# A decode of float64 weights with one Vector instruction fewer, and a hand-over between two MLPs begun earlier, in a fused attention and MLP kernel

## The chip, the cores and the metric

One core of one Trainium2 chip runs the whole program. The metric is the device time of one execution in microseconds. The engines are named as in the profile: PE is the matrix engine, DVE the vector engine, ACT the scalar engine, POOL the GpSimd engine, and SP the engine that does nothing here but issue DMAs. Each of them works through its own list of instructions strictly in the written order, so an instruction that waits holds back all that is written behind it on its engine.

## The reference

A softmax attention without a score matrix feeds two MLPs. Weights arrive as float64; activations are float32.

```python
def _attn_ref(q, k, v):                 # 8 batches, 8 heads, 576 tokens, 64 wide
    q_s = softmax over the last axis of q
    k_s = softmax over the tokens of k
    kv = np.einsum('bhsd,bhse->bhde', k_s, v)
    return np.einsum('bhsd,bhde->bhse', q_s, kv)

def _moe_ref(x, w_gate, w_val, w_out, rms_g):   # 4608 tokens, 512 -> 1536 -> 512
    xn = x / np.sqrt(np.mean(x * x, axis=-1, keepdims=True) + 1e-06) * rms_g
    g = xn @ w_gate
    return (g * (1 / (1 + np.exp(-g))) * (xn @ w_val)) @ w_out

def _moe2_ref(x, w_in, w_out):                  # 4608 tokens, 512 -> 2048 -> 512
    h = x @ w_in
    return (h * (1 / (1 + np.exp(-1.702 * h)))) @ w_out
```

## The kernel before

**Stages.** (1) The attention of the first batch and the first weights. (2) Nine tiles of 512 tokens through the first MLP (index j); inside each tile the attention of later batches is woven in. A tile has 36 slots, three for each of the 12 blocks of the hidden width: a gate product, a value product, and an output product of the block before. (3) The first product of the second MLP (`in_round`): six units of 768 tokens, four rounds each. (4) Its second product: nine groups of 512 tokens, eight steps of the hidden width each; the loop over `k` counts all 72. The products of the second MLP are done with seven instead of eight block products, so each operand is first turned into seven sums and differences (`sums`, line 570), and each of the seven is split into a high and a low part: ACT copies the high part, DVE or POOL subtracts to get the low one.

**Decoding.** A weight is a float64, read as two 32 bit words. `decode` (lines 136 to 157) takes the absolute value of the high word on ACT (line 148), scales the low word on ACT (149), then on DVE clips from below (150), shifts left by three and masks (151), and puts sign and top bit back (154); POOL adds the low word (157). There are 68 pieces of 128x512. `advance` decodes 36 of them, three before and 33 during tile 0, beside which POOL also makes the low parts (line 161). A piece passes through one of three `stage` buffers; its next fetch is issued by SP only when POOL has added the low word. The other 32 pieces, for the second MLP, are decoded in tiles 1 to 7 (`decode_aside`) and parked in DRAM.

**Order in tile 0.** In the DVE list decoding stands between the attention's steps. The step that matters to PE is line 411 (`qL`): it reads a PSUM bank that PE's transpose at line 328 waits for, and behind that transpose stand the output product (line 526) and all that follows.

**The hand-over from stage 3 to stage 4.** `beside[i, t]` holds what is to be done after PE's block number t of unit i. In the last unit (END) the factors of step k=0 (`u2_split(0)`) are made after block 25: ACT copies the high part (line 739) out of `aside`, DVE subtracts (742). They lie where the factors of the first five of a round's seven block products lay (`pools["x"]`), which are last read in block 25. Block 26 and 27 follow with two additions on DVE, two GELUs on ACT and two stores on SP each. Only then come the loads of step 3 and of the last weights (`y`), the sums of step 1, and its split. The data of steps 4 and 5 are loaded behind those.

**The end.** The last group's four tiles of 128 tokens are y2 (i = 0, 1) and y1 (i = 0, 1). DVE finishes them with seven additions, and DMAs store whole rows of 512.

Of the kernel before, what the change touches and what calls it, by code (L numbers as in the profile page):

```python
# [20 lines left out]
def attention_glu_mlp(  # L21
# [90 lines left out]
    def f(x):  # L112
        return x.bitcast(F32)
# [22 lines left out]
    def decode(name, dst):  # L136

        st = stages.pop(name)
        lo, hi = st[:, :, 0], st[:, :, 1]


        nc.scalar.activation(f(dst), f(hi), AF.Abs)
        nc.scalar.activation(lo, lo.bitcast(U32), AF.Copy, scale=2.0**-29)
        nc.vector.tensor_scalar_max(f(dst), f(dst), 2.0**-15)  # L150
        nc.vector.tensor_scalar(  # L151
            dst, dst, 3, 0x3FFFFFF8, op0=ALU.logical_shift_left, op1=ALU.bitwise_and
        )
        nc.vector.scalar_tensor_tensor(
            out=dst, in0=hi, scalar=-0x40000000, in1=dst, op0=ALU.bitwise_and, op1=ALU.bitwise_or
        )
        return lambda: nc.gpsimd.tensor_tensor(dst, dst, lo, op=ALU.add)  # L157

# [475 lines left out]
        halve(w[:, 0], w[:, 1], xraw2[i, c][:, RIGHT[p]], nc.vector)  # L634
        xfac[i, p, c] = w

    def in_round(i, q, after):


        sets = (2 * q, 2 * q + 1)  # L640
        st = {m: {} for m in sets}

        def gelu(m, k, dst, src):
            nc.scalar.activation(dst, src, AF.Gelu_apprx_sigmoid)  # L644
            nc.sync.dma_start(out=u2_d[i][m][:, k], in_=dst)

        def room():
            return pools["h"].tile([P, W], F32, tag="h", bufs=12, name="h")

        for p in ORDER:  # L650
            for s, m in enumerate(sets):
                d = st[m]
                if p in (1, 6, 5):
                    d[p] = pools["ps"].tile([P, 512], F32, tag="bank", bufs=8, name="ps_in")
                t = d[{1: 1, 2: 1, 6: 6, 7: 6, 4: 6, 5: 5, 3: 5}[p]][:, 0:W]
                w = wpack["2i", q, p]
                for c in range(2):
                    for k, (a, e) in enumerate(PASSES):
                        nc.tensor.matmul(  # L659
                            t,  # L660
                            w[:, a, s, c * P : (c + 1) * P],
                            xfac[i, p, c][:, e, :],
                            start=p in (1, 6, 5) and c == 0 and k == 0,
                            stop=c == 1 and k == 2,
                            skip_group_check=True,
                        )
                if p == 1:
                    d["c1"] = room()
                    nc.scalar.activation(d["c1"], t, AF.Copy)
                elif p == 6:  # L670
                    d["u2"] = room()
                    nc.vector.tensor_tensor(d["u2"], d["c1"], t, op=ALU.add)
                elif p == 2:
                    gelu(m, 2, room(), t)
                elif p == 7:
                    d["u3"] = room()
                    nc.vector.tensor_tensor(d["u3"], d["c1"], t, op=ALU.add)
                else:
                    k, name = {5: (1, "u3"), 4: (3, "c1"), 3: (0, "u2")}[p]
                    v = d[name]  # L680
                    nc.vector.tensor_tensor(v, v, t, op=ALU.add)  # L681
                    gelu(m, k, v, v)
            after(ORDER.index(p))
# [3 lines left out]
        unit, o = divmod(2 * g + i, W // P)  # L687
        return unit, o * P, (2 * unit + h) * W + o * P

    def store_out(first, y, queue=nc.scalar):  # L690

        done = 0
        while done < P:
            b, o = divmod(first + done, S)
            rows = sum(halves_of(b), [])
            while o >= size(rows[0]):
                o -= size(rows.pop(0))
            m = min(P - done, size(rows[0]) - o)
            if rows[0] < R - 1:
                dst = out[b * S : b * S + FULL].rearrange("(p r) e -> r p e", p=P)[rows[0]]  # L700
            else:
                dst = out[b * S + FULL : (b + 1) * S]
            queue.dma_start(out=dst[o : o + m, :], in_=y[done : done + m, :])
            done += m


# [22 lines left out]
        if k in uraw:  # L729
            sums(uraw[k], "A", (nc.vector,) * 4)  # L730

    def u2_split(k, ahead=True):

        if k not in uraw:
            return
        raw = uraw.pop(k)[:, 1:8]
        pool, bufs = (pools["u"], 2) if k % 3 < 2 else (pools["d"], 1)
        w = pool.tile([P, 2, 7, Q], F32R, tag="uf", bufs=bufs, name="uf")
        nc.scalar.activation(w[:, 0], raw, AF.Copy)  # L739
        if ahead:  # L740
            u2_sums(k + 1)
        nc.vector.tensor_tensor(w[:, 1], raw, f(w[:, 0]), op=ALU.subtract)  # L742
        ufac[k] = w

    def warm(func):

# [3 lines left out]
    with tc.manual_schedule():  # L750
# [187 lines left out]
            pools["x"].release()  # L938
            pools["u"] = tc.alloc_tile_pool(name="u2p", bufs=1, side="right", reuse_waits="tile")

        beside[END, 25].insert(0, free_x)
        beside[END, 25].insert(1, lambda: u2_split(0, False))
        put2(END, 25, lambda: u2_load(2))
        for i in range(NUNIT):
            for q in range(4):

                def after(k):
                    for fn in beside.pop((i, 7 * q + k), ()):
                        fn()

                in_round(i, q, after)


        pools["h"].release()
# [4 lines left out]

            return dpool.tile([P, 8, Q], F32, tag="y", bufs=2, name="y")  # L960

        assert not beside
        u2_load(3)

        work = {}
        for m in (6, 7):
# [2 lines left out]

            for k, part in ((m - 4, a[1:2]), (2 * m - 9, a[2:6]), (2 * m - 8, a[6:])):  # L970
                work.setdefault(k, []).extend(part)
        u2_sums(1)
        u2_split(1, False)
        u2_sums(2)
        for k in range(4, 6):
            u2_load(k)
        stores = []
        for k in range(NT // T * NSET):
            g, m = divmod(k, NSET)
# [22 lines left out]
            for p in (1, 6, 7, 5, 3, 4, 2):  # L1002
# [21 lines left out]
                elif p == 6:  # L1024
                    add(u2, c1)
                elif p == 7:
                    add(u3, u2)
                elif p == 5:
                    add(y2[:, :, 0:Q], u3)
                    add(u2, u2)  # L1030
                    u2_split(k + 2)
                    u2_load(k + 6)
                elif p == 3:
                    add(u2, u2)
                elif p == 4:
                    add(u3, u3)
                    if end:
                        for i in range(2):
                            store_out(first_token(g, i, 0)[2], y2[:, i, :], nc.sync)
                else:  # L1040
                    add(c1, c1)
            if last:
                for h, y in ((0, y2), (1, y1)):
                    for i in range(2):
                        if h or not end:
                            queue = nc.sync if end and i else nc.scalar
                            stores.append(
                                lambda i=i, h=h, y=y, g=g, queue=queue: store_out(
                                    first_token(g, i, h)[2], y[:, i, :], queue
                                )  # L1050
                            )
        for fn in stores:
            fn()
        dpool.release()
        pools["u"].release()
        pools["raw"].release()
# [40 lines left out]
```

## Time and profile before

| | us |
|---|---|
| median of three runs (lowest to highest) | 1777.21 (1776.85 to 1777.32) |
| the profiled execution, own time | 1777.49 |
| its span in the trace | 1775.7 |
| PE busy, DVE busy, ACT busy, POOL busy | 1726.4, 1174.9, 770.7, 378.3 |
| PE busy in the first 45.5 us | 22.3 |
| PE idle ahead of the second MLP's output products (line 1007), in all | 7.0 |
| end of PE's last matmul | 1768.5 |
| ACT on a piece: line 148 and line 149, mean | 0.667, 0.666 |
| DVE's line 154 in tile 0, shortest and longest | 0.69, 1.67 |
| an addition of line 681 and a GELU of line 644, mean | 0.553, 0.525 |

The profile shows one execution. A row of a view gives the source line, the engine, the instruction and what it wrote and read; the time in square brackets is how long the engine had been idle before it, and what ended that. The same instruction can be busy for quite different times: line 151 takes 0.43 us in most rows of one kind of piece and 1.39 us in all of the other.

### The profile page before, as it was taken

Reading aid. Unit: us, or ns where it says so; the run is one execution under the profiler, and the core shown is the slowest. Engines: PE = TensorE matmul, PEld = TensorE weight load, DVE = VectorE, ACT = ScalarE, POOL = GpSimd, SP = SyncE. Lnnn points to the kernel's source line nnn. Section 1 sums busy time; section 2 is a strip of 40 time slices with the busy share of each in tenths; the row PEclk is TensorE's granted clock in tenths of the full one; section 3 lists DMA queues with packets and bytes.
Section 4 is the critical chain, followed back from the end, with each engine's and each line's share of the span. In section 5 each row is a group of like instructions: output and inputs, shape, how many; then the busy total and the mean of one; then the engine's idle time right before and its main releaser. Section 6 shows DMA issues by size and latency. Waiting matters only on the chain.

```text
span 1775.7 us, 26550 instructions
## 1 busy us (share of the span) xinstructions
PE 1726.4 (97%) x10044; PEld 1523.8 (86%) x10044; DVE 1174.9 (66%) x1995; ACT 770.7 (43%) x1290; POOL 378.3 (21%) x352
## 2 busy tenths in 40 slices
PE   5889999999999999999999999999999999999998
PEld 3556788888888888888888889999999899999998
DVE  7999775757757577574224367545556897777785
ACT  4666444444444444443122245444445533333332
POOL 4666222122222212211112523000003540000000
PEclk8899999999999999999999999999999999999999
DMA  5455322323223232120001134443444544444432
GB/s 160 130 173 160 111 86 64 109 58 116 76 74 100 65 109 76 62 59 1 24 1 48 43 122 145 143 143 111 145 146 166 194 130 132 131 123 128 131 119 84
DMA packets 202000, 186.30 MB, mean 105 GB/s; under 512 B 58256, under 2 KB 183696, under 8 KB 201872
## 3 DMA queue, kind: packets, MB, share of 16 engines
q1 hardware_dynamic: 192176, 167.03, 30.7%
q10 hardware_dynamic: 9696, 17.57, 2.7%
q8 instruction: 79, 1.29, 0.3%
q14 instruction: 49, 0.40, 0.1%
HBM read 119.54 MB, written 65.01 MB: 104 GB/s over the span
## 4 chain that ended last, share of the span: by engine, by line
PE 88%; DVE 6%; issue 1%; DMA 1%; SPq 1%; ACT 1%; POOL 1%; DVEq 0%; POOLq 0%
PE ps_gv L496 30%; PE ps_in L659 20%; PE ps_out L1007 18%; PE ps_acc L496 15%; PE ps_acc L526 1%; DVE uf L742 1%; PE ps_att L374 1%; PE ps_att L402 1%; DVE raw L570 1%; DMA stage<-in_moe_w_out_dram 1%; DVE w L151 0%; DVE raw L151 0%; SPq L271 0%; PE ps_att L452 0%; DVE w L150 0%
## 5 line engine op out<-in xcount | busy, mean ns | idle before, releaser
L1007 PE MATMUL ps_out<-w2o,uf 128*128 128x256 f32 x3024 | 365.5, 284 | 7.0 <-DVE uf L742 3.8
L1007 PEld LDWEIGHTS ps_out<-w2o,uf 128*128 128x128 f32 x3024 | 363.8, 192 | 8.6 <-DVE uf L742 4.4
L659 PE MATMUL ps_in<-xf,w2i 128*128 128x384 f32 x2016 | 349.9, 334 | 0.8 <-DVE ev L547 0.8
L659 PEld LDWEIGHTS ps_in<-xf,w2i 128*128 128x128 f32 x2016 | 349.4, 188 | 1.4 <-DVE ev L547 1.2
L496 PE MATMUL ps_gv<-xs,wg 128*128 128x512 f32 x1296 | 323.9, 399 | 2.3 <-ACT xs L487 1.5
L496 PE MATMUL ps_gv<-xs,wv 128*128 128x512 f32 x1296 | 316.9, 393 | 1.0 <-POOL wv L161 0.7
L496 PEld LDWEIGHTS ps_gv<-xs,wg 128*128 128x128 f32 x1296 | 242.9, 190 | 60.3 <-issue 3.2
L496 PE MATMUL ps_acc<-u,wo 128*128 128x512 f32 x1152 | 283.8, 395 | 0.0
L496 PEld LDWEIGHTS ps_gv<-xs,wv 128*128 128x128 f32 x1296 | 239.1, 188 | 49.6 <-POOL wv L161 2.1
L496 PEld LDWEIGHTS ps_acc<-u,wo 128*128 128x128 f32 x1152 | 212.0, 188 | 44.6
L848 ACT ACTIVATE s<-ps_gv 128x512 f32<-128x512 f32 x108 | 64.6, 598 | 420.4 <-PE ps_gv L496 420.2
L161 POOL TENSOR_TENSOR wo<-raw,wo 128x512 fp32r<-128x512 f32 x96 | 124.0, 1292 | 491.7 <-ACT wo L160 450.8
L854 DVE TENSOR_TENSOR s<-s,ps_gv 128x512 f32<-128x512 f32 x108 | 73.9, 684 | 193.8 <-PE ps_gv L496 174.5
L644 ACT ACTIVATE h<-h 128x384 f32<-128x384 f32 x144 | 74.4, 525 | 115.4 <-DVE h L681 91.5
L157 POOL TENSOR_TENSOR w<-w,stage 128x512 int32<-128x512 int32 x56 | 73.3, 1310 | 213.0 <-PE ps_att L419 100.0
L570 DVE TENSOR_TENSOR raw<-raw 128x256 f32<-128x256 f32 (+1 forms) x236 | 108.9, 503 | 9.5 <-DMA raw<-w2d 7.5
L681 DVE TENSOR_TENSOR h<-h,ps_in 128x384 f32<-128x384 f32 x144 | 78.0, 553 | 49.4 <-PE ps_in L659 48.4
L739 ACT ACTIVATE uf<-raw 128x1792 fp32r<-128x1792 f32 x36 | 61.3, 1701 | 90.1 <-PE ps_out L1007 59.6
L742 DVE TENSOR_TENSOR uf<-raw,uf 128x1792 fp32r<-128x1792 f32 x36 | 74.4, 2067 | 20.3 <-ACT uf L739 20.3
L574 POOL TENSOR_TENSOR w2o<-raw,w2o 128x256 fp32r<-128x256 f32 x35 | 28.2, 841 | 276.0 <-DMA u<-h 270.2
L365 DVE TENSOR_REDUCE qs<-qe 128x10 f32<-128x640 f32 x32 | 26.3, 820 | 85.6 <-ACT qe L359 85.5
L574 DVE TENSOR_TENSOR xf<-raw,xf 128x384 fp32r<-128x384 f32 x84 | 43.8, 567 | 39.7 <-ACT xf L573 39.7
(144 smaller groups left out, 1914.9 us busy)
## 6 DMA issues: line engine op xcount, KB each, us to landing
u<-h SPq DMA_DIRECT2D x192, 192.0 KB, 1.9
stage<-in_moe_w_out_dram SPq DMA_DIRECT2D x28, 512.0 KB, 3.6
raw<-u SPq DMA_DIRECT2D x24, 512.0 KB, 4.2
x<-ev ACTq DMA_DIRECT2D x34, 256.0 KB, 2.0
stage<-in_moe_w_in_dram SPq DMA_DIRECT2D x16, 512.0 KB, 3.8
w2d<-w SPq DMA_DIRECT2D x32, 256.0 KB, 3.0
v_sb<-in_v_dram SPq DMA_DIRECT2D x60, 128.0 KB, 3.2
out_dram<-y ACTq DMA_DIRECT2D x30, 256.0 KB, 4.3
```

The lines of the kernel that those rows point to most:

```text
L157: return lambda: nc.gpsimd.tensor_tensor(dst, dst, lo, op=ALU.add)
L161: nc.gpsimd.tensor_tensor(dst[:, 1, :], src, f(dst[:, 0, :]), op=ALU.subtract)
L496: nc.tensor.matmul(t, w(a), x(e), start=first and i == 0, stop=last and i == 2)
L570: engine.tensor_tensor(raw[:, o], raw[:, a], raw[:, b], op=op)
L574: engine.tensor_tensor(dst_l, src, f(dst_h), op=ALU.subtract)
L644: nc.scalar.activation(dst, src, AF.Gelu_apprx_sigmoid)
L659: nc.tensor.matmul(t, w[:, a, s, c * P : (c + 1) * P], xfac[i, p, c][:, e, :], start=p in (1, 6, 5) and c == 0 and k == 0, stop=c == 1 and ...
L681: nc.vector.tensor_tensor(v, v, t, op=ALU.add)
L742: nc.vector.tensor_tensor(w[:, 1], raw, f(w[:, 0]), op=ALU.subtract)
L848: nc.scalar.activation(s, tg, AF.Silu)
L854: nc.vector.tensor_tensor(s, s, tv, op=ALU.mult)
L1007: nc.tensor.matmul(t[:, i * Q : (i + 1) * Q], u[:, a, LEFT[p] - 1, i * P : (i + 1) * P], w[:, e, m % 2, :], start=m == 0 and i == 0 and n ...
```

## The change

Decode: the absolute value is scaled by 2^-112 on ACT, the clip goes, and the shift stands alone without a mask. The last DVE instruction keeps only the sign bit of the high word instead of its top two bits.

Hand-over: `u2_split` is cut into `u2_high` (ACT) and `u2_low` (DVE). `u2_high(0)` is put inside block 25, behind its matmuls and ahead of the second set's addition and GELU; the sums, the high part of step 1 and the load of step 3 move in between blocks 26 and 27.

End: the last group's stores are cut in halves of 256 columns, each issued as soon as its addition is written, for i=0 by SP and for i=1 by ACT.

```diff
-        nc.scalar.activation(f(dst), f(hi), AF.Abs)
+        nc.scalar.activation(f(dst), f(hi), AF.Abs, scale=2.0**-112)
         nc.scalar.activation(lo, lo.bitcast(U32), AF.Copy, scale=2.0**-29)
-        nc.vector.tensor_scalar_max(f(dst), f(dst), 2.0**-15)
-        nc.vector.tensor_scalar(
-            dst, dst, 3, 0x3FFFFFF8, op0=ALU.logical_shift_left, op1=ALU.bitwise_and
-        )
+        nc.vector.tensor_single_scalar(dst, dst, 3, op=ALU.logical_shift_left)
         nc.vector.scalar_tensor_tensor(
-            out=dst, in0=hi, scalar=-0x40000000, in1=dst, op0=ALU.bitwise_and, op1=ALU.bitwise_or
+            out=dst, in0=hi, scalar=-0x80000000, in1=dst, op0=ALU.bitwise_and, op1=ALU.bitwise_or
         )
...
+                if s:
+                    between(ORDER.index(p))
                 if p == 1:
...
-    def u2_split(k, ahead=True):
+    def u2_high(k):
+
+        pool, bufs = (pools["u"], 2) if k % 3 < 2 else (pools["d"], 1)
+        w = ufac[k] = pool.tile([P, 2, 7, Q], F32R, tag="uf", bufs=bufs, name="uf")
+        nc.scalar.activation(w[:, 0], uraw[k][:, 1:8], AF.Copy)
+
+    def u2_low(k):
+        raw, w = uraw.pop(k)[:, 1:8], ufac[k]
+        nc.vector.tensor_tensor(w[:, 1], raw, f(w[:, 0]), op=ALU.subtract)
+
+    def u2_split(k):
...
+        u2_high(k)
+        u2_sums(k + 1)
+        u2_low(k)
...
-        beside[END, 25].insert(0, free_x)
-        beside[END, 25].insert(1, lambda: u2_split(0, False))
+        midway = {(END, 25): (free_x, lambda: u2_high(0))}
+        beside[END, 25].insert(0, lambda: u2_low(0))
         put2(END, 25, lambda: u2_load(2))
+        put2(END, 26, lambda: u2_sums(1), lambda: u2_high(1), lambda: u2_load(3))
...
-        u2_load(3)
...
-        u2_sums(1)
-        u2_split(1, False)
-        u2_sums(2)
         for k in range(4, 6):
             u2_load(k)
+        u2_low(1)
+        u2_sums(2)
...
-                    if end:
-                        for i in range(2):
-                            store_out(first_token(g, i, 0)[2], y2[:, i, :], nc.sync)
...
-            if last:
+                if end and p in (5, 3, 4, 2):
+                    h, y = (0, y2) if p in (5, 4) else (1, y1)
+                    part = slice(0, Q) if p in (5, 3) else slice(Q, DM)
+                    for i, queue in enumerate((nc.sync, nc.scalar)):
+                        store_out(first_token(g, i, h)[2], y[:, i, :], queue, part)
+            if last and not end:
```

Line numbers of the kernel after differ by a few; the names are the same. The first place is DVE's list in tile 0, from the sum over a query's exponentials (`qs`) to the `qL` that PE waits for; `raw` and `w` are pieces being decoded. Before:

```order
L367 RECIPROCAL qs<-qs 128x10
L150 TENSOR_SCALAR raw_838<-raw_838 128x512
L151 TENSOR_SCALAR raw_838<-raw_838 128x512
L154 SCALAR_TENSOR_TENSOR raw_838<-stage,raw_838 128x512
...
L150 TENSOR_SCALAR w_994<-w_994 128x512
L151 TENSOR_SCALAR w_994<-w_994 128x512
L154 SCALAR_TENSOR_TENSOR w_994<-stage,w_994 128x512
L321 TENSOR_REDUCE m_1010<-k_sb 128x128
L150 TENSOR_SCALAR w_1012<-w_1012 128x512
L151 TENSOR_SCALAR w_1012<-w_1012 128x512
L154 SCALAR_TENSOR_TENSOR w_1012<-stage,w_1012 128x512
L411 TENSOR_TENSOR qL<-ps_att,qH 128x320
```

The same place of the kernel after, in which line 150 is the shift:

```order
L364 RECIPROCAL qs<-qs 128x10
L150 TENSOR_SCALAR raw_828<-raw_828 128x512
L151 SCALAR_TENSOR_TENSOR raw_828<-stage,raw_828 128x512
...
L150 TENSOR_SCALAR w_980<-w_980 128x512
L151 SCALAR_TENSOR_TENSOR w_980<-stage,w_980 128x512
L318 TENSOR_REDUCE m_995<-k_sb 128x128
L150 TENSOR_SCALAR w_997<-w_997 128x512
L151 SCALAR_TENSOR_TENSOR w_997<-stage,w_997 128x512
L408 TENSOR_TENSOR qL<-ps_att,qH 128x320
```

Each piece has two rows instead of three; nothing else in the list moved, and the lists of PE and POOL are the same in both kernels.

The second place is ACT's list at the hand-over: `h<-h` are the GELUs of blocks 25 to 27, `uf<-aside` the high part of step 0, `uf<-raw` that of steps 1 and 2. Before:

```order
L644 ACTIVATE h<-h 128x384 x2
L739 ACTIVATE uf<-aside 128x1792
L573 ACTIVATE w2o_3_12370<-raw 128x256
L644 ACTIVATE h<-h 128x384 x4
L739 ACTIVATE uf<-raw 128x1792 x2
```

After:

```order
L641 ACTIVATE h<-h 128x384
L735 ACTIVATE uf<-aside 128x1792
L641 ACTIVATE h<-h 128x384
L570 ACTIVATE w2o_3_12302<-raw 128x256
L641 ACTIVATE h<-h 128x384 x2
L735 ACTIVATE uf<-raw 128x1792
L641 ACTIVATE h<-h 128x384 x2
L735 ACTIVATE uf<-raw 128x1792
```

Step 0's copy passes one GELU and step 1's passes two; on SP the load of step 3 (`ur`) passes the two stores of block 27 in the same way, and on DVE the sums of step 1 pass block 27's two additions.

The third place is the end of SP's list, the stores of the output. Before:

```order
L722 DMA raw<-u_5_6_162 128x4x256
L722 DMA ur<-u_5_7_163 128x4x256
L703 DMA out_dram<-y 64x512 x2
L703 DMA out_dram<-y 128x512 x2
L1092 UNCONDITIONAL_BRANCH
```

After:

```order
L721 DMA raw<-u_5_6_162 128x4x256
L721 DMA ur<-u_5_7_163 128x4x256
L702 DMA out_dram<-y 64x256 x2
L702 DMA out_dram<-y 128x256
L702 DMA out_dram<-y 64x256 x2
L702 DMA out_dram<-y 128x256
L1097 UNCONDITIONAL_BRANCH
```

SP has six stores of half rows instead of four of whole rows, and ACT four (128x256) instead of one (128x512).

## Rows read from the trace of the kernel before

**Rows 1.** Tile 0, 45.5 to 183.2 us: busy time by engine, granted clock, DMA.
```profile
45.50:183.20 137.70, 127.01 (x521) 84.62 (x522) 131.21 (x187) 89.84 (x152) 88.60 (x66) 0.93 0.51 156
```

**Rows 2.** Lines 150, 151, 154 in that stretch: DVE sums, then durations min/median/max.
```profile
45.50:183.20 137.70, 23.79 (x33) 0.93 0.51 156
45.50:183.20 137.70, 33.32 (x33) 0.93 0.51 156
45.50:183.20 137.70, 33.43 (x33) 0.93 0.51 156
L150 DVE TENSOR_SCALAR w<-w x21: 412/529/1501, 48.7 to 168.3; 128x512 f32<-128x512 f32 x21
L151 DVE TENSOR_SCALAR w<-w x21: 426/428/1417, 49.8 to 168.7; 128x512 int32<-128x512 int32 x21
L151 DVE TENSOR_SCALAR raw<-raw x12: 1375/1390/1440, 53.7 to 176.1; 128x512 int32<-128x512 int32 x12
```

**Rows 3.** Waits, 40 to 185 us: of PE, and one of ACT: us, times, longest.
```profile
PE ps_att L328 <- DVE qL L411: 6.6, 3, 2.5
PE ps_att L340 <- DVE m L332: 2.6, 1, 2.6
PE ps_gv L496 <- POOL wg L161: 0.8, 1, 0.8
PE ps_gv L496 <- POOL wv L161: 0.7, 2, 0.4
ACT raw L148 <- DMA stage<-in_moe_w_out_dram: 13.1, 6, 3.0
```

**Rows 4.** PE in tile 0 in order of time.
```profile
77.08 5.30 PE L526 MATMUL ps_acc<-s,raw 128*128 128x512 f32 x8
...
89.47 3.70 PE L526 MATMUL ps_acc<-s,raw 128*128 128x512 f32 x8
...
153.02 2.56 PE L496 MATMUL ps_gv<-xs,wg 128*128 128x512 f32 x10 [0.79 <-POOL wg L161]
```

**Rows 5.** Busy times of a window of 2 us; the 0.56 is the granted clock.
```profile
78.00:80.00 2.00, 2.00 (x4) 0.81 (x3) 1.93 (x3) 1.57 (x3) 1.26 (x1) 0.56 0.42 116
```

**Rows 6.** The chain that ended last, ahead of PE's wait at 101.2 us.
```profile
90.26 0.29 DVE raw L150
...
90.58 1.41 DVE raw L151
...
95.82 0.78 DVE w L150
...
99.00 0.47 DVE w L150
```

**Rows 7.** The hand-over, 1390 to 1450 us, in order of time.
```profile
1393.12 1.69 ACT L739 ACTIVATE uf<-aside 128x1792 fp32r<-128x1792 f32 x1
...
1398.10 3.00 SPq L645 DMA_DIRECT2D u<-h  x4
...
1404.58 0.53 SPq L722 DMA_DIRECT2D aside<-u  x1
...
1406.43 2.10 DVE L570 TENSOR_TENSOR ur<-ur 128x256 f32<-128x256 f32 x4 [0.99 <-DMA ur<-u]
...
1410.93 2.50 DVE L570 TENSOR_TENSOR aside<-aside 128x256 f32<-128x256 f32 x4
...
1448.63 11.54 PE L1007 MATMUL ps_out<-w2o,uf 128*128 128x256 f32 x94 [2.96 <-DVE y L1021]
```

**Rows 8.** DMA issues from 1402 to 1408 us: step 4's load, us to landing.
```profile
aside<-u SPq DMA_DIRECT2D x1, 512.0 KB, 6.3
```

**Rows 9.** The end: the additions and SP's stores in order of time.
```profile
1765.01 4.86 DVE L1021 TENSOR_TENSOR y<-y,ps_out 128x512 f32<-128x512 f32 x7 [7.78 <-PE ps_out L1007]
1769.29 2.48 SPq L703 DMA_DIRECT2D out_dram<-y  x4
```

**Rows 10.** A window of 1 us at the end: DMA share and GB/s stand last.
```profile
1772.00:1773.00 1.00, 0.00 (x0) 0.00 (x0) 0.00 (x0) 0.00 (x0) 0.00 (x0) 0.50 0.98 352
```

More of the change, by code (lines that the diff above doesn't have):

```diff
@@ L635, in x2_split, with in_round @@
         xfac[i, p, c] = w
-    def in_round(i, q, after):
+    def in_round(i, q, after, between):
         sets = (2 * q, 2 * q + 1)
@@ L688, in first_token, with store_out @@
         return unit, o * P, (2 * unit + h) * W + o * P
-    def store_out(first, y, queue=nc.scalar):
+    def store_out(first, y, queue=nc.scalar, part=slice(0, DM)):
         done = 0
@@ L702, in store_out @@
                 dst = out[b * S + FULL : (b + 1) * S]
-            queue.dma_start(out=dst[o : o + m, :], in_=y[done : done + m, :])
+            queue.dma_start(out=dst[o : o + m, part], in_=y[done : done + m, part])
             done += m
@@ L730, in u2_sums @@
             sums(uraw[k], "A", (nc.vector,) * 4)
-    def u2_split(k, ahead=True):
+    def u2_high(k):
[6 more added lines that the diff above has]
+    def u2_split(k):
         if k not in uraw:
             return
[L736 to L743, printed above, removed]
+        u2_high(k)
+        u2_sums(k + 1)
+        u2_low(k)
     def warm(func):
@@ L949, in after, with between @@
                         fn()
-                in_round(i, q, after)
+                def between(k):
+                    for fn in midway.pop((i, 7 * q + k), ()):
+                        fn()
+                in_round(i, q, after, between)
         pools["h"].release()
@@ L960, in y_tile @@
             return dpool.tile([P, 8, Q], F32, tag="y", bufs=2, name="y")
-        assert not beside
-        u2_load(3)
+        assert not beside and not midway
         work = {}
@@ L1036, in attention_glu_mlp @@
                     add(u3, u3)
-                    if end:
-                        for i in range(2):
-                            store_out(first_token(g, i, 0)[2], y2[:, i, :], nc.sync)
                 else:
                     add(c1, c1)
-            if last:
+                if end and p in (5, 3, 4, 2):
[4 more added lines that the diff above has]
+            if last and not end:
                 for h, y in ((0, y2), (1, y1)):
                     for i in range(2):
[L1045 to L1050, printed above, removed]
-                            )
-        for fn in stores:
-            fn()
+                        stores.append(
+                            lambda i=i, h=h, y=y, g=g: store_out(
+                                first_token(g, i, h)[2], y[:, i, :]
+                            )
+                        )
         dpool.release()
```

## Prediction, made before the kernel after had run

> **What bounds the kernel now.** I read the busy times first: PE is busy for 1726 of 1776 us, so a gain can come only from where PE stands still or runs at the low clock. Nearly all of its 49 us of standing lies in four places: 23.2 in the first 45.5 us (attention alone), 10.7 in tile 0, 7.0 at the hand-over near 1400 us, and 7.2 after its last matmul (the profile table). The change touches all four. Tiles 1 to 7, where the other 32 pieces are decoded, have a PE that is always busy; what DVE saves there is worth nothing.
>
> In tile 0 DVE is the bound: 131.2 of 137.7 us busy, PE 127.0 at a mean clock of 0.93 [rows 1]. PE's waits there are few and long: three at the transpose behind `qL` (6.6 us), one at line 340 (2.6), three for POOL's low parts (0.8 and 0.7) [rows 3], together 10.7. Each of the first four costs a second time: the output product behind the wait takes 5.30 us where it takes 3.70 elsewhere [rows 4], and the granted clock just then is 0.56, that is mostly the 1.2 GHz level [rows 5]. After the wait of 0.79 us ten matmuls took 2.56 us, 0.256 each, so that wait brought no low clock [rows 4]. The stretch therefore holds 10.7 + 4 x 1.6 = 17.1 us that PE could get back.
>
> The hand-over holds 7.0 us of PE idle time (the profile table), of which the last wait of 2.96 us, for a DVE that is behind with its additions, is the one that ends the stretch [rows 7]. At the end, PE has stopped and the stores run out.
>
> **The change part by part.** The profiled execution took 1777.49 us; it lies 0.28 above the median, and the sum is made against it.
>
> *Decode.* Each piece loses the clip. ACT's absolute value keeps its kind of instruction; line 149 already scales, and costs ACT the same 0.67 us as the unscaled line 148 (the table), so I add nothing. The shift alone has no row. Its nearest rows are the two others of its kind: a clip with one operation takes 0.412 at least, a shift with mask 0.426 [rows 2]; I take 0.43 and no change for it, its bounds being 0.41 and, held, 1.39.
> The 33 clips of tile 0 sum to 23.8 us, 0.72 each [rows 2]. That is not all gain: unhindered a clip takes 0.41, and the rest is time in which it is held. That time goes with POOL: on raw pieces, where POOL's low parts run beside it, line 151 always takes 1.38 or more, on the others 0.43 [rows 2]. Take the clip away and its successor may be held instead. So a clip on the path is worth 0.41 to 0.72.
> How many are on the path? Between the query sums, which ACT releases, and the `qL` that PE waits for there are three, of 0.29, 0.78 and 0.47 us [rows 6], 1.54 together; bounds 1.2 (three of 0.41) and 2.2 (the whole mean wait, 6.6 / 3). I take 1.5. Then 0.7 of the 2.2 us is left, less than the 0.79 that brought no low clock, so the product behind it should take 3.7 again. Three such places: 3 x 1.5 = 4.5, and 3 x 1.6 = 4.8 of clock.
> At the first wait (line 340) two clips lie ahead: 0.8. It keeps 1.8 us, nearer to the 2.2 than to the 0.79, so its clock stays low. In the last 30 us POOL's three waits, 1.5 together, depend on the same DVE list; I take half, 0.75. Before tile 0 three pieces are decoded, and I count one clip of 0.4 there.
> Sum: 0.4 + 0.8 + 4.5 + 4.8 + 0.75 = **11.25 us**. Bounds: 0.4 + 0.8 + 3 x 1.2 + 0.5 = 5.3 if the clock falls as before; 17.1 + 0.4 = 17.5 if PE never waits.
>
> *Hand-over.* Step 0's copy stands ahead of one GELU (ACT now does it at 1393.12 [rows 7]), so the low part of step 0 and all DVE work behind it start earlier by the addition and the GELU passed, 0.55 + 0.53 (the table), and step 1's sums stand ahead of two additions. Moved ahead with them is the load of step 3, past two stores that wait on SP for their GELUs (the four store issues stretch over 3.0 us); for this load DVE waited 0.99 us [rows 7]. What is late next is the load of step 4, issued at 1404.58 and landing 6.3 us later [rows 8], at 1410.9, exactly when its sums begin at 1410.93 [rows 7]. It still stands behind the last stores and the `y` loads. Its landing shortens only by what is no longer in the queue ahead of it: half a megabyte (step 3) of about 2.25 (step 3, 1 MB of `y`, itself, and a part of step 5), an estimate of 6.3 x 0.5 / 2.25 = 1.4 us. Of the moved GELUs' stores nobody is in haste but the tile of step 2's factors, which lies over their buffers: DVE could go about 3 us earlier, the loads allow 1.4. I take **2.0 us**, nearer the load's. From there to 1448.63 DVE runs without a pause, so PE's last wait ends that much earlier. Bounds: 7.0 (all of PE's idle time) and -2.0, if step 4's load, behind later stores, lands later by the same size.
> The GELU that step 0's copy passes is 1.7 us later; behind it waits only its store.
>
> *End.* DVE's last addition ends at 1765.01 + 4.86 = 1769.87 [rows 9]. Before, SP starts issuing at 1769.29 and ends its fourth at 1771.77 [rows 9], 0.6 us for each. Now the halves of two additions go out before 1769.3, SP's last is held only by the two half stores ahead of it, and issues at about 1770.5 (two issues of 0.6 after 1769.3), ending at 1771.1 at the latest; halves that cross no more rows than before should issue a little faster, and half the bytes are under way earlier. I take **1.0 us**. Bounds 0 (the same bytes at the same rate) and 1.9 (the last issue at once, 1771.77 - 1769.87).
> The DMA engines were 0.98 busy in the middle of the stores [rows 10], which speaks for the small end. The Trainium skill (DMA: Bandwidth & Descriptors, Issuing engines are not separate DMA queues) says that transfers issued from several engines run on the same 16 DMA engines, and that issuing from several saves only issue time. By that rule the use of ACT's queue is worth issue time alone; no row here separates the two, and the sum stays.
>
> Together 11.25 + 2.0 + 1.0 = 14.25 us: 1777.49 - 14.25 = **1763.2 us**.
>
> **The rivals.**
> *The low clock stays.* The shortened waits of about 1 us still bring the low clock; 11.25 becomes 5.3. 1777.49 - 8.3 = 1769.2. For it: between 0.79 and 2.0 us of waiting no row says which way it goes.
> *PE becomes the bound.* All 23.8 us leave DVE's list, more than the 17.1 PE lacks. 17.5 + 3.0: 1757.0. For it: DVE is busy nearly throughout. Against: part of the 23.8 is held time that moves on.
> *The fetches are the bound.* A stage buffer goes round from fetch through ACT, DVE and POOL. ACT already waited 13.1 us for raw pieces [rows 3]. If DVE only takes over that wait at the three places, 0.4 + 0.8 + 0.75 = 2 us remain: 1777.49 - 5.0 = 1772.5. Against: POOL, which frees the buffer, waits for DVE's last step.
> *Slower: POOL's holds fall on both steps that are left.* Now a piece costs DVE (23.8 + 33.3 + 33.4) / 33 = 2.74 us. If the new rhythm puts a POOL instruction ahead of every shift and every last step, they take 1.39 [rows 2] and 1.67 (the table): 3.06, or 0.32 x 33 = 10.5 us more in tile 0. 1777.49 + 10.5 - 3.0 = 1785.0. It decides from 2.83 us a piece (3.0 / 33 above 2.74) on. Against: 21 of 33 pieces now have an unheld shift at the median, and POOL's work did not grow.
> The Trainium skill (SBUF — State Buffer, SBUF: two separate sides) has a port pair shared by DVE and GpSimd that one instruction locks for its whole duration while the other blocks. Rows 2, with 0.43 and 1.39 for one instruction, agree; the rule makes the handed-on hold likelier than a saving of all 23.8 us.
> *The change does less than it says:* decode gains as in the first rival, and hand-over and end give nothing or lose: 1772 to 1776. It is counted with the fetches.
>
> **How the numbers follow.** Forecast 1763.2, its own range 1759 to 1767: 0.50. Low clock stays (1767 to 1771): 0.22. PE the bound (1755 to 1759): 0.15. Fetches (1771 to 1775.5): 0.08. No change: 0.02. Slower: 0.03. A measurement of this kernel can tell about 0.2%, 3.5 us, from no change. Up to 1773.9 it counts as faster: the first three and two thirds of the fetches, 0.92. Same: 0.05. Slower: 0.03. The range leaves out the slow end from 1770.5 on (0.13 with the cases behind it, and a little of the low-clock case) and the fastest 0.05: **1756.5 to 1770.5**.
>
> **What would show it.** Tile 0 should end 10 to 11 us earlier, at about 172; PE's three waits behind `qL` should be under 1 us each, and the products behind them 3.7 us. Waits of 1 us with products of 5.3 show the first rival; ACT's waits for fetches passed on to DVE show the third; shifts of 1.39 us on most pieces the fourth. At the hand-over step 3's sums should start without a wait, step 4's load land near 1409 on the old scale, and the last wait be over 2 us earlier. From PE's last matmul to the end it should take 6.2 us instead of 7.2. The forecast is wrong if the shift alone takes another time than 0.43, or if DVE in tile 0 gains and PE's waits stay.

## The result, and the profile after

The changed kernel takes 1760.66 us (median of four runs, 1758.79 to 1762.46). The kernel before took 1777.26 beside it (1776.85 to 1778.12). The ratio is 0.9906, with an interval of 0.9889 to 0.9923: 16.6 us faster. The forecast was 1763.2, and the range of 1756.5 to 1770.5 holds the time. Each of its three terms is nevertheless 1 to 4 us from what its stage shows.

The profiled execution after took 1760.03 us, 17.46 less than the one before. PE's rows in order of time split that by stage:

| Stage | before | after | difference |
|---|---|---|---|
| until tile 0's first gate product | 45.49 | 44.45 | -1.04 |
| from there to the second MLP's first output product | 1350.52 | 1335.58 | -14.94 |
| hand-over, to the end of its last wait | 52.62 | 51.62 | -1.00 |
| from there to PE's last matmul | 319.86 | 321.31 | +1.45 |
| PE's last matmul to the end of the span | 7.21 | 5.24 | -1.97 |
| outside the span | 1.79 | 1.83 | +0.04 |

**Tile 0** gives most of the second line: to the next tile's first gate product it takes 122.8 us, where the kernel before takes 137.2 (the window of [rows 1] ends half a us later). These are its busy times in the kernel after, then DVE's sums of the shift (line 150) and of the last step (line 151); then durations in ns (minimum, median and maximum) of the shift on both kinds of piece and of the output product; then PE's waits, and last the gate product behind the first wait, before and after.

```profile
44.45:167.25 122.80, 119.68 (x520) 81.19 (x521) 114.15 (x155) 90.03 (x152) 93.71 (x66) 0.98 0.57 174
```

```profile
44.45:167.25 122.80, 25.49 (x33) 0.98 0.57 174
...
44.45:167.25 122.80, 46.17 (x33) 0.98 0.57 174
```

```profile
L150 DVE TENSOR_SCALAR w<-w x21: 411/753/1530, 47.7 to 151.4; 128x512 int32<-128x512 int32 x21
L150 DVE TENSOR_SCALAR raw<-raw x12: 364/729/1369, 51.2 to 157.7; 128x512 int32<-128x512 int32 x12
...
L523 PE MATMUL ps_acc<-s,raw x88: 590/592/697, 61.7 to 167.2; 128*128 128x512 f32 x88
```

```profile
PE ps_att L337 <- DVE m L329: 1.2, 2, 0.9
PE ps_gv L493 <- POOL wv L158: 1.0, 2, 0.7
PE ps_att L325 <- DVE qL L408: 0.8, 1, 0.8
```

```profile
56.78 4.59 PE L496 MATMUL ps_gv<-xs,wg 128*128 128x512 f32 x12
...
54.34 3.01 PE L493 MATMUL ps_gv<-xs,wg 128*128 128x512 f32 x12
```

Where before DVE was busy for 131 us and PE for 127 [rows 1], now PE is the busier, with 3.0 us of waits left of 10.7 [rows 3]. The two steps that stay cost (25.49 + 46.17) / 33 = 2.17 us a piece, where the three took 2.74. The rows of a piece are thus only 0.57 us shorter, not the clip's 0.72: the last step rose from 33.43 [rows 2] to 46.17, while the shift fell from 33.32 to 25.49. Part of the held time (what an instruction takes above its shortest) moved on. In all, the decode's rows lose 18.9 us; DVE's other instructions take 2.3 us longer, DVE stands still for 2.2 us more, and tile 0 is 14.4 us shorter. No output matmul exceeds 697 ns, so none ran at the low clock; before, three groups of eight took 5.1 to 5.3 us instead of 3.7 [rows 4], and twelve gate products 4.59 instead of 3.01.

**The hand-over**, in order of time: ACT's last two GELUs, the issue of their stores, the `y` loads, step 2's copy, step 4's load, and what DVE and PE wait for; then, from SP's own list of waits, how long the `y` loads waited for those stores, after and before.

```profile
1382.27 1.70 ACT L735 ACTIVATE uf<-raw 128x1792 fp32r<-128x1792 f32 x1 [0.94 <-DVE raw L567]
...
1383.88 0.92 ACT L641 ACTIVATE h<-h 128x384 f32<-128x384 f32 x2
...
1384.41 0.79 SPq L642 DMA_DIRECT2D u<-h  x2
1385.29 4.59 SPq L593 DMA_DIRECT2D y<-w2d  x4
...
1386.08 5.06 PE L1014 MATMUL ps_out<-w2o,uf 128*128 128x256 f32 x40 [0.63 <-DVE uf L739]
1388.56 1.56 DVE L567 TENSOR_TENSOR ur<-ur 128x256 f32<-128x256 f32 x4 [1.07 <-DMA ur<-u]
1389.64 1.70 ACT L735 ACTIVATE uf<-raw 128x1792 fp32r<-128x1792 f32 x1 [4.85 <-DMA y<-w2d]
1389.93 0.53 SPq L721 DMA_DIRECT2D aside<-u  x1
...
1393.73 1.57 PE L1014 MATMUL ps_out<-w2o,uf 128*128 128x256 f32 x7 [1.83 <-DVE uf L739]
1394.89 1.56 DVE L567 TENSOR_TENSOR aside<-aside 128x256 f32<-128x256 f32 x4 [1.21 <-DMA aside<-u]
...
1431.65 30.57 PE L1014 MATMUL ps_out<-w2o,uf 128*128 128x256 f32 x240 [2.57 <-DVE y L1028]
```

```profile
SPq L593 <- DMA u<-h: 2.1, 1, 2.1
...
SPq L596 <- DMA u<-h: 0.6, 1, 0.6
```

Put on the old scale (16.0 us later, so that the first output products coincide), step 4's load is issued at 1405.9 and its sums begin at 1410.9: later than, and at the same time as, before [rows 7]. Step 3's sums still wait for their load, 1.07 us where they waited 0.99. PE resumes step 1 2.0 us earlier than before, but step 2, whose copy on ACT stands still for 4.85 us, only 1.35, and at the end of the last wait 1.0 is left.

**Behind the last wait** 1.45 us were lost. These windows of 2 us show PE after that wait, first after, then before; the third number from the end is the granted clock.

```profile
1432.00:1434.00 2.00, 2.00 (x11) 2.00 (x11) 1.97 (x6) 0.00 (x0) 0.00 (x0) 0.50 0.59 172
```

```profile
1448.00:1450.00 2.00, 1.37 (x11) 1.37 (x12) 2.00 (x4) 0.00 (x0) 0.00 (x0) 1.00 0.13 33
```

After, the clock is at 0.50, the 1.2 GHz level; before it stood at 1.00 after a longer wait.

**The end**: the additions, the stores' issues, and (second fence) KB and time to landing of the stores there.

```profile
1749.47 4.86 DVE L1028 TENSOR_TENSOR y<-y,ps_out 128x512 f32<-128x512 f32 x7 [7.78 <-PE ps_out L1014]
1751.77 3.74 SPq L702 DMA_DIRECT2D out_dram<-y  x6
1751.78 2.94 ACTq L702 DMA_DIRECT2D out_dram<-y  x4
```

```profile
out_dram<-y ACTq DMA_DIRECT2D x4, 128.0 KB, 2.1
out_dram<-y SPq DMA_DIRECT2D x4, 64.0 KB, 2.3
out_dram<-y SPq DMA_DIRECT2D x2, 128.0 KB, 2.3
```

SP's last issue ends 2.55 us after PE's last matmul (before: 1771.77 - 1768.50 = 3.27), and the rest to the end of the span is 2.7 us (before: 3.9).

### The profile page after: what moved, and what is told of

Read it like the earlier page. It is cut to its first block, busy times and chain, and to the rows that moved or that the text cites. A ratio compares the mean times of both kernels' runs of the same rounds, so it can differ in the third digit from the quotient of the medians.

```text
span 1758.2 us, 26492 instructions
## 1 busy us (share of the span) xinstructions
PE 1721.4 (98%) x10044; PEld 1523.5 (87%) x10044; DVE 1139.4 (65%) x1927; ACT 770.4 (44%) x1290; POOL 382.4 (22%) x352
## 4 chain that ended last, share of the span: by engine, by line
PE 94%; DVE 4%; ACT 1%; issue 1%; DMA 1%; POOL 0%; SPq 0%; DVEq 0%; ACTq 0%; POOLq 0%
PE ps_gv L493 33%; PE ps_out L1014 20%; PE ps_in L656 20%; PE ps_acc L493 15%; PE ps_acc L523 2%; PE ps_att L371 1%; PE ps_att L399 1%; PE ps_att L449 0%; PE ps_att L414 0%; PE ps_att L416 0%; PE ps_att L415 0%; DVE y L1028 0%; DVE qs L362 0%; DVE m L318 0%; DVE w L151 0%
## 5 line engine op out<-in xcount | busy, mean ns | idle before, releaser
L510 DVE TENSOR_TENSOR u<-s,u 128x512 fp32r<-128x512 f32 x96 | 68.1, 709 | 3.3
```

The source lines that it names most:

```text
L510: nc.vector.tensor_tensor(u[:, 1, :], s, f(u[:, 0, :]), op=ALU.subtract)
```

## The experiments

Letters of theories count within one expectation only.

### Each part alone

Decode alone, from the changed kernel: hand-over and end as before the change. Its main lines against the kernel before:

```diff
-        nc.vector.tensor_scalar_max(f(dst), f(dst), 2.0**-15)
...
-            dst, dst, 3, 0x3FFFFFF8, op0=ALU.logical_shift_left, op1=ALU.bitwise_and
...
+        nc.vector.tensor_single_scalar(dst, dst, 3, op=ALU.logical_shift_left)
```

> The decode of the kernel after alone; hand-over and end as before. By the trace of the kernel after, tile 1 starts 15.4 us earlier: theory A (the decode carries the gain) expects 1777.3 - 15.4 = 1762 us, within 1.5. The forecast's sum expects 11.25, that is 1766. Rival B (part of the earlier tile 1 is given back in the second MLP) expects 1764 or more.

Hand-over alone, the old decode and the old end:

```diff
+        midway = {(END, 25): (free_x, lambda: u2_high(0))}
...
+        put2(END, 26, lambda: u2_sums(1), lambda: u2_high(1), lambda: u2_load(3))
```

> The hand-over of the kernel after alone; decode and end as before. Theory A (the load of step 4 and step 2's copy still wait for the last GELU stores to land) expects no gain: 1776.5 to 1778. The forecast's sum expects 2.0 us: 1775.3.

End alone, the old decode and the old hand-over:

```diff
+                    for i, queue in enumerate((nc.sync, nc.scalar)):
+                        store_out(first_token(g, i, h)[2], y[:, i, :], queue, part)
```

> The half-row stores of the last group alone; decode and hand-over as before. Theory A, by the 5.24 us from PE's last matmul to the end in the kernel after against 7.2: 1775.3. The forecast's sum: 1776.3. If the bytes and not the issue bounded the end: 1777.3.

Decode and end, the old hand-over:

```diff
-        midway = {(END, 25): (free_x, lambda: u2_high(0))}
...
-        put2(END, 26, lambda: u2_sums(1), lambda: u2_high(1), lambda: u2_load(3))
```

> The kernel after with the hand-over of before. Theory A: the same as the kernel after within 1 us, 1759.5 to 1761. The forecast's sum: 2.0 us above the kernel after, 1762.7. If the hand-over does harm through the low clock seen twice in the trace of the kernel after (0.83 in two windows of 10 us): 1 to 1.5 us below it, 1759.3.

| Kernel | us (lowest to highest) | ratio to before [95%] |
|---|---|---|
| before, beside these | 1777.96 (1775.56 to 1779.50) | |
| decode alone | 1762.76 (1761.68 to 1763.34) | 0.9913 [0.9896, 0.9929] |
| hand-over alone | 1776.42 (1774.41 to 1778.66) | 0.9990 [0.9981, 1.0000] |
| end alone | 1775.94 (1774.78 to 1777.47) | 0.9988 [0.9978, 0.9997] |
| decode and end | 1760.74 (1759.24 to 1761.35) | 0.9900 [0.9885, 0.9915] |

Decode is worth 15.2 us, not 11.25. The end is worth 2.0, alone and on top of decode (1762.76 - 1760.74). The hand-over is worth 1.5 us alone, between its two theories, with an interval that touches no change, and nothing on top of the other two: 0.9906 with it, 0.9900 without. From PE's last matmul to the end the traces give 7.17 and 7.19 us with the old stores and 5.24 and 5.22 with the new.

### How decode's gain depends on the clips

In the next two a clip that changes no value is put back, on one kind of piece each:

```diff
+        if name[0] == "o":
+            nc.vector.tensor_scalar_max(f(dst), f(dst), 0.0)
         nc.vector.tensor_single_scalar(dst, dst, 3, op=ALU.logical_shift_left)
```

> The changed kernel with a clip (a maximum with zero, which changes no value) back on the 11 pieces of the output weight of tile 0 alone; the 22 gate and value pieces go without. Theory A (each clip on DVE's list is worth the same, 15.2 us over 33): a third of the gain goes, 5.1 us, 1765.8 us. Theory B (the last clips count double, since they bring back the waits behind the line of qL and with them the low clock of the output products): 8 to 10 us slower, 1769 to 1771 us, with output products of 5.3 us back. Theory C (the first clips removed give all, since PE is the limit after them): under 2 us slower.

```diff
+        if name[0] in "gv":
+            nc.vector.tensor_scalar_max(f(dst), f(dst), 0.0)
         nc.vector.tensor_single_scalar(dst, dst, 3, op=ALU.logical_shift_left)
```

> The changed kernel with a clip (a maximum with zero, which changes no value) back on the 22 gate and value pieces alone. With the clip on the 11 output pieces the kernel lost 5.2 us, 0.47 us a clip. Theory A (each clip on DVE's list costs the same): 10.4 us slower than the changed kernel, 1771 us. Theory B (a threshold: the low clock comes back with the first clips): the two parts don't add up to the 15.2 us of the whole, 12 us or more here, 1773 us; or 7 us or less, 1768 us, where the output pieces sit closer to the waits.

There are 12 output pieces and 24 gate and value pieces, three of these ahead of tile 0; the counts of 11, 22 and 33 in the expectations are off. The first took 1765.93 us (ratio 0.9930 [0.9914, 0.9947]), the second 1770.87 (0.9956 [0.9941, 0.9971]). Against the changed kernel's 1760.66 that is 5.3 / 12 = 0.44 us a clip and 10.2 / 24 = 0.43; the whole gain is 15.2 / 36 = 0.42. The ratios, each to the kernel before beside it, would give 0.36 and 0.37 for the two; the traces decide for the first reckoning. The second tile starts at 166.6 to 167.8 us in the seven profiles with the changed decode (mean 167.1), at 172.4 and 177.3 in these two, and at 182.0 to 182.8 in the three with the old decode: 5.3 / 12 = 0.44, 10.2 / 24 = 0.43 and 15.4 / 36 = 0.43 us a clip. So theory A holds in both: the gain is linear, and a clip is worth about what it takes unheld, 0.41 [rows 2].

PE's waits in tile 0 with the clip on the output pieces, and the output product's durations:

```profile
PE ps_att L339 <- DVE m L331: 4.2, 4, 1.8
PE ps_att L327 <- DVE qL L410: 3.1, 3, 1.4
...
L525 PE MATMUL ps_acc<-s,raw x88: 590/592/697, 61.7 to 172.3; 128*128 128x512 f32 x88
```

The same with the clip on the gate and value pieces:

```profile
PE ps_att L327 <- DVE qL L410: 4.4, 3, 2.0
PE ps_att L339 <- DVE m L331: 2.8, 3, 2.2
...
L525 PE MATMUL ps_acc<-s,raw x88: 590/592/1061, 63.2 to 177.3; 128*128 128x512 f32 x88
```

With 12 clips there are again waits of up to 1.8 us, but no output product at the low clock; with 24 the 1.06 us product is back. The time knows nothing of that step: it rises by 0.43 to 0.44 us a clip in both. So tile 0's length follows DVE's list, and I conclude that the low clock of a product ran in time that PE would otherwise have waited.

The mask alone put back, the clip still gone:

```diff
-        nc.vector.tensor_single_scalar(dst, dst, 3, op=ALU.logical_shift_left)
...
+            dst, dst, 3, 0x7FFFFFF8, op0=ALU.logical_shift_left, op1=ALU.bitwise_and
```

> The changed kernel with the mask back in the shift (two operations in one instruction, as before the change), clip still gone. Theory A (the clip alone carries the gain; shift and last step share their held time whatever the shift does): shift and last step together stay near 2.0 to 2.2 us a piece, 1760 to 1762 us. Theory B (the shift without its mask saves 0.24 us a piece, 25.5 against 33.3 us over tile 0, at the price seen before the change): 4 to 8 us slower than the changed kernel, 1765 to 1769 us.

1761.28 us (0.9903 [0.9888, 0.9918]), the changed kernel's time, as theory A had it. DVE's sums of the shift with mask and of the last step in tile 0:

```profile
43.70:167.26 123.56, 26.76 (x33) 0.98 0.56 173
...
43.70:167.26 123.56, 46.14 (x33) 0.98 0.56 173
```

26.8 + 46.1 = 72.9 us beside 71.7 without the mask: the mask is worth nothing that can be told from zero, and the clip is the whole gain. That the shift fell from 33.3 to 25.5 us is not the mask's going either.

The last step left out, so that every weight counts as positive:

```diff
-        nc.vector.scalar_tensor_tensor(
-            out=dst, in0=hi, scalar=-0x80000000, in1=dst, op0=ALU.bitwise_and, op1=ALU.bitwise_or
-        )
```

> The changed kernel without the last DVE step of a piece, the one that puts the sign back, so that every weight is taken as positive: that part of the computation is left out. DVE loses 46 us of 114 us of tile 0's stretch of 123 us. Theory A (PE is now the limit there, with some 3 us of waits for DVE and POOL left): 1 to 4 us faster than the changed kernel, 1757 to 1760 us. Theory B (DVE still sets the pace of tile 0): 10 us or more faster, under 1751 us.

1755.60 us (0.9874 [0.9859, 0.9888]). Tile 0:

```profile
43.20:162.86 119.66, 118.28 (x520) 81.51 (x521) 69.37 (x122) 89.70 (x152) 87.06 (x66) 0.98 0.58 179
```

DVE drops from 114 to 69 us, and the stretch only from 122.8 to 119.7, of which PE is busy for 118.3. The median is 5.1 us lower than the changed kernel's, a little more than theory A's 1 to 4. In the profiles 1.2 of it lies ahead of tile 0 (where the kernels with the changed decode differ by as much among themselves, 43.2 to 44.5), 3.1 in tile 0, and 1.46 behind the hand-over, where this execution has no low clock. So in tile 0 PE is all but the limit of the changed kernel: giving up 45 us of DVE's work brings 3.1 us there.

### What holds the hand-over

The tile of step 2's factors taken ahead of the `y` tiles, step 3's load issued before the GELUs, and step 4's load ahead of the `y` loads:

```diff
+        first_uf.append(dpool.tile([P, 2, 7, Q], F32R, tag="uf", bufs=1, name="uf"))
...
+        midway = {(END, 25): (free_x, lambda: u2_high(0), lambda: u2_load(3))}
...
+        u2_load(4)
```

> The changed kernel with three moves at the hand-over: the tile of step 2's factors is taken from its pool ahead of the y tiles, so that its copy waits for no store of block 27's GELUs; the load of step 3 is issued before block 27's GELUs, and the load of step 4 ahead of the two y loads that wait for those stores. Theory A (the landing of block 27's GELU stores, 4.4 to 4.7 us, holds step 2's copy and, through the queue on SP, the load of step 4): the waits of 1.8 and 0.3 us before step 2 and part of the last one of 2.6 us go, 2 to 3 us in all, 1758 us where the changed kernel has 1760.7. Theory B (DVE's chain of sums and subtractions is the limit, stores or not): the waits move to the next step, within 1 us of the changed kernel. Theory C (the last wait, for the first y load, stands whatever comes before it): earlier work of PE only lengthens that wait, 1760 to 1761 us, with the last wait at 4 us or more.

1759.30 us (0.9892 [0.9877, 0.9906]). PE in the hand-over:

```profile
1386.95 10.68 PE L1020 MATMUL ps_out<-w2o,uf 128*128 128x256 f32 x84 [0.63 <-DVE uf L744]
1397.79 20.41 PE L1020 MATMUL ps_out<-w2o,uf 128*128 128x256 f32 x168 [0.16 <-DVE uf L744]
...
1430.98 24.18 PE L1020 MATMUL ps_out<-w2o,uf 128*128 128x256 f32 x187 [2.96 <-DVE y L1034]
```

The waits of 1.83 and 0.26 us are gone, and the stretch takes 50.08 us, the shortest of all. But 0.16, 0.58 and 0.21 us at later steps stand in their place, and the last wait is 2.96, as in the kernel before: theory A for step 2, while neither its shorter last wait nor theory C's 4 us came.

Only the tile moved:

```diff
+        first_uf.append(dpool.tile([P, 2, 7, Q], F32R, tag="uf", bufs=1, name="uf"))
```

> The changed kernel with the tile of step 2's factors taken from its pool ahead of the y tiles, and nothing else; the loads of steps 3 and 4 stay where the change has them. In the run with all three moves this hand-over, from its first output product to the end of its last wait, took 50.1 us where the changed kernel has 51.6. Theory A (what held step 2 was its copy, whose tile lies over the buffers of block 27's GELUs): the waits of 1.8 and 0.3 us before step 2 go as in that run, and the hand-over takes 50 to 50.5 us, 1759.3 us in all. Theory B (the load of step 4 behind the y loads on SP is the gate): the wait moves on to step 3 or 4, the hand-over stays at 51.3 us or more, 1760.5 us.

1761.18 us (0.9905 [0.9888, 0.9921]): theory A fell, and theory B held. The `y` loads, which now wait for the stores from the first on, step 4's sums, and PE:

```profile
1389.43 1.75 SPq L593 DMA_DIRECT2D y<-w2d  x4
...
1391.22 0.53 SPq L721 DMA_DIRECT2D aside<-u  x1
...
1396.89 1.55 DVE L567 TENSOR_TENSOR aside<-aside 128x256 f32<-128x256 f32 x4 [4.92 <-DMA aside<-u]
...
1400.44 1.87 PE L1020 MATMUL ps_out<-w2o,uf 128*128 128x256 f32 x7 [3.12 <-DVE uf L744]
```

Step 2 waits only 0.90 us, but step 4's load, behind the `y` loads on SP, is 1.3 us later still, and PE now waits 3.12 us before step 3. The stretch took 53.87 us. Tile and queue both hang on the same stores: by SP's list of waits the `y` loads waited 4.3 us for them here, 2.1 in the changed kernel.

Only step 0's copy early; the sums and copy of step 1 and step 3's load back behind the loop:

```diff
-        put2(END, 26, lambda: u2_sums(1), lambda: u2_high(1), lambda: u2_load(3))
```

> The changed kernel with only step 0's copy begun inside the last round; the sums and the copy of step 1 and the load of step 3 are back behind the loop. Theory A (what the early work of step 1 gains is lost again before step 2, where the landing of the stores decides): the hand-over, from its first output product to the end of its last wait, takes 51.5 to 52 us as in the changed kernel, within 0.5 us of 1760.7 us. Theory B (the early work of step 1 is worth what it moves): the wait before step 1 is back at 1.5 us where the changed kernel has 0.6, a hand-over of 52.3 to 52.6 us, 1761.5 us.

1758.88 us (0.9890 [0.9875, 0.9904]), lower than either theory had it:

```profile
1380.02 1.92 ACT L641 ACTIVATE h<-h 128x384 f32<-128x384 f32 x4 [1.84 <-DVE h L680]
...
1380.76 2.52 SPq L642 DMA_DIRECT2D u<-h  x4
...
1386.69 5.29 PE L1016 MATMUL ps_out<-w2o,uf 128*128 128x256 f32 x42 [1.56 <-DVE uf L739]
1387.22 0.53 SPq L721 DMA_DIRECT2D aside<-u  x1
...
1388.18 1.70 ACT L735 ACTIVATE uf<-raw 128x1792 fp32r<-128x1792 f32 x1 [3.61 <-DMA y<-w2d]
...
1393.44 1.82 PE L1016 MATMUL ps_out<-w2o,uf 128*128 128x256 f32 x13 [1.46 <-DVE uf L739]
```

This names the cause (the first output products of the two profiles lie 0.3 us apart). Without step 1's copy between them the four GELUs run in one piece, 1380.02 to 1381.94. In the changed kernel that copy of 1.70 us stands ahead of the last two, which end at 1384.80. The stores are all issued by 1383.28 instead of 1385.20, and step 4's load at 1387.22 instead of 1389.93. PE waits 1.56 us before step 1 where the changed kernel waits 0.63, and 1.46 before step 2 where that waits 1.83 + 0.26. The stretch takes 51.30 us. Of the 0.93 us that step 1 gains from its early copy, 0.63 is paid before step 2 by the stores that this copy delays, and step 4's load is 2.4 us later: theory A, and a little more.

The stretch varies from one execution to another: 51.9 to 52.6 us in the four profiles with the old hand-over (mean 52.3), 51.6 to 53.3 in the seven with the new (mean 52.4). That is the hand-over's gain: none that can be told from zero.

One row sets its end. From the end of step 4's sums to the end of the last wait it takes 35.2 us in thirteen of the fourteen profiles (35.7 with the earlier loads), and DVE has no wait in between. What PE gains at steps 1 to 3, or loses there to the low clock, therefore does not count; only earlier sums of step 4 do. With the old hand-over their load is issued 8.3 to 8.6 us after the first output product and they never wait for it; with the new one it is issued at 9.9 to 10.5, and they wait 1.0 to 2.7 us for it, in all seven. Where it goes out at 7.5 (only step 0's copy early) and 5.3 (the earlier loads), the sums end earlier than in any of those eleven.

### The end

The last stores as whole rows, still spread over both queues:

```diff
-                if end and p in (5, 3, 4, 2):
+                if end and p in (4, 2):
...
-                        store_out(first_token(g, i, h)[2], y[:, i, :], queue, part)
+                        store_out(first_token(g, i, h)[2], y[:, i, :], queue)
```

> The changed kernel with the last four stores as whole rows, begun when both halves of a row are summed, each pair still spread over the queues of SP and ACT. In the changed kernel the span ends 5.2 us after PE's last matmul, in the kernel before 7.2 us. Theory A (the halves count: the last store is smaller and the others start earlier, and landing takes 2.2 us where it took 3 to 3.4): 7 us from the last matmul to the end, 1762.5 us. Theory B (the spread over two queues and the order of the last sums carry the gain): 5.2 to 6 us, 1760.7 to 1761.4 us.

1761.49 us (0.9905 [0.9890, 0.9920]); its median cannot tell 1.6 us from nothing, but its trace can: 6.86 us from PE's last matmul to the end, where the ten traces with the halves give 5.14 to 5.28.

```profile
out_dram<-y ACTq DMA_DIRECT2D x2, 256.0 KB, 2.9
out_dram<-y SPq DMA_DIRECT2D x2, 128.0 KB, 3.6
out_dram<-y SPq DMA_DIRECT2D x1, 256.0 KB, 3.8
```

Theory A: the halves carry it. The last issue ends 0.64 us later, and landing takes 2.9 to 3.8 us instead of 2.1 to 2.3. Halves are both smaller and begun earlier; no run separates the two. The Trainium skill (DMA: Bandwidth & Descriptors, Issuing engines are not separate DMA queues) lets a second issuing engine save issue time only; the run agrees as far as it goes, since both queues kept gave only 0.3 us (7.2 to 6.86) without the halves.

## Why the prediction was right, and where it was not

- *Total*: right, partly by luck, since the errors cancel in part: decode 4 us too small, hand-over 2 too large, end 1 too small, and in the profiled execution 1.45 lost behind the hand-over.
- *Decode, 11.25 against 15.2.* The bound was named rightly (DVE), but the term was then counted at single waits of PE: three clips ahead of each, plus the clock of the product behind. The step that failed is "How many are on the path?". All 36 clips turned out to be on the path, at about their unheld 0.41 each: 36 x 0.41 = 14.8. Both prices stood in the prediction, and the lower one fits the time. It is a fit: the decode's rows themselves lost 0.57 a clip, and the rest went into DVE's other instructions and waits. At PE, the forecast's own place of counting, the shortfall is 1.3 us at the waits behind `qL` (5.8 gone, not 4.5), 0.6 at line 340 and 1.6 for the low clock behind it, and 0.6 ahead of tile 0. The Trainium skill (SBUF — State Buffer, SBUF: two separate sides) has a port pair of DVE and GpSimd locked by one instruction at a time; the last step's rise from 33.4 to 46.2 us agrees with it, and no run here took POOL's work away to test it.
- *The clock as a term of its own, 4.8.* The three output products did come back at 3.7 us, as forecast. But as a gain beside the clips it failed: the kernel with 12 clips has no low-clock output product and costs its 12 clips all the same. At the first wait (line 340) the forecast kept 1.8 us and the low clock; two waits of 1.2 us together are left, and no low clock. (What ran low behind that wait before was a gate product, not an output product, as the prediction had it.)
- *The rivals for decode.* "The low clock stays" fell. "PE becomes the bound" is half true: PE is now all but the limit in tile 0, with 3.0 us of waits left, but its time of 1757.0 took in a hand-over that did not come. "Fetches" and "slower" fell: 2.17 us a piece, far from the 2.83 where the loss would begin.
- *The shift's 0.43.* True as the minimum (0.41 and 0.36), not as the mean (25.49 / 33 = 0.77); the rest is held. By the prediction's own sign of being wrong this counts against it.
- *Hand-over, 2.0 against none.* The step that failed is the sentence that nobody is in haste for the moved GELUs' stores but step 2's tile, by which the loads were taken as the limit: the `y` loads wait for the same stores, and step 4's load stands behind them on SP. "The GELU that step 0's copy passes is 1.7 us later; behind it waits only its store" overlooked the same thing for step 1's copy. So the load was issued 1.3 us later instead of landing 1.4 earlier; the prediction had this path only as its lower bound. That step 4's sums decide, and that DVE then runs without a pause, was right. Step 3's sums were to start without a wait and waited 1.07 us.
- *End, 1.0 against 2.0.* The sums and issues came as worked out (0.7 of issue); landing was taken as unchanged, and the half-size stores let the span end 1.2 us sooner after the last issue. The upper bound of 1.9 was about right.

The kernels with only step 0's copy early (1758.88) and with the earlier loads (1759.30) have lower medians than the changed kernel and ratios of 0.9890 and 0.9892 against its 0.9906. They beat the kernel before; the intervals overlap the change's, and whether they beat it is open. The two ideas were not put together.

## What to carry to other kernels

Where one engine bounds a whole stage, count an edit at all its instructions, up to the slack of the next engine; the unheld duration was the price that fitted here. Don't count it at single waits, and don't add the clock's loss that hides in them. Before moving work ahead on an in-order engine, list what the passed instruction releases, down to the last buffer and queue: here a GELU 2 us later held its store, the store held a tile and two loads, and these held a third load. And on the final stores it was the cutting into halves that mattered, not the spread over two queues.

## What the runs showed of the hardware

- The same wait is followed by different clocks. The last wait of the hand-over was 2.96 or 2.97 us in eleven of the fourteen profiles. In three of these (the kernel before among them) the granted clock stays at 1.00, and from its end to PE's last matmul it takes 319.9 us; in six one drop to the 0.50 level follows and it takes 321.0 to 321.3; in the two of hand-over and end alone it takes 322.3. So a drop costs 1.4 us and a longer one 2.4, whatever the change did; the length of the wait does not decide it, and what does is open. The profile of the kernel before, on which the sum was made, was one without it.
- Waits of up to 1.8 us in tile 0 brought no low clock (clip on the output pieces). With the clip on the others, the granted clock stayed at 1.00 behind the wait of 2.2 us (55 to 70 us) and fell to 0.50 behind one of 2.0 (123 to 125). At the hand-over, the granted clock behind the wait of 1.83 us before step 2 was 0.53 (1394 to 1396 us of the kernel after); with the hand-over alone, 1.84 us there brought no drop.
- Removing a step of 0.72 us made the last step of the piece 0.39 us longer (46.17 - 33.43 = 12.74, over 33) and the step between 0.24 shorter. A duration that includes holding is not a price.
